# A three-pass mixture of experts on one core: splits of pass 1 put a step later, operands of pass 3 made in pass 2

## Chip, cores and metric

The kernel runs on one core of one Trainium2 chip. The metric is the time of one execution on the device in microseconds (us), lower is better. Before the change it is 2345.62 us, the median of 3 runs (2342.83 to 2346.38).

## What is computed

Attention with a threshold, a gated feed-forward block, and a mixture of eight experts whose gate is normalised over rows and columns eight times. The change concerns the experts alone.

```
attn = softmax(where(scores >= max - tau, scores, -1e9)) @ v
x = (silu(attn @ w_gate) * (attn @ w_val)) @ w_out
P = exp(x @ w_gate2 - max); 8 times: P /= row sums; P /= column sums; P *= N / E
out = sum over e of P[:, e] * (relu(x @ w1[e]) @ w2[e])
N, D, E, F = 2304, 512, 8, 1024
```

## The kernel before

Every product is made of three matmuls in a fast fp32 format: an operand is split into a high half (a copy, on ScalarE) and a low half (the operand less its high half, on GpSimd or VectorE), and high x high, high x low and low x high are added up.

The experts' part runs over the 2304 tokens in three passes (`u` = 0, 1, 2), of two blocks of 384 tokens each. The text calls them pass 1, 2 and 3. A pass has 32 steps (`k`): each takes 256 of the 1024 hidden columns of one of the 8 experts, four steps to an expert (`PAIRS` = 4). In a step the 2 x 2 product of weights and x is made as seven products of sums of quarters. They stand in the order `UP_ORDER` = (1, 2, 6, 5, 7, 4, 3), and the number n of a product names the slot of the step.

Pass 1 (the loop over k from L1664) makes the weights' operands as it goes and stores them in DRAM for passes 2 and 3. `a_steps(k + 1)` makes those of w1 for the next step: three sums on VectorE, then the splits `wa` and `wb`, then s4 (L1095), which writes over a part of what `wa` was made of and so must wait for GpSimd's low half of `wa`, then the split `wc` of s4. `b_steps(k)` splits w2, `t_sums(k)` makes four differences of w2 on VectorE, and `t_steps(k)` splits these a step later, with one low half on GpSimd and one on VectorE. `a_store`, `b_store` and `t_store` write the operands to DRAM. Meanwhile TensorE does the seven up-products of step k (`up`, six matmuls of 384 columns each) and, between them, the products with w2 of step k - 1 (`mix`, six pieces of six matmuls of 512 columns, called y-matmuls here), whose results VectorE adds to the output tiles `acc`. Product 6 is copied to `av` by ScalarE, product 7 to `u3`; products 6, 7 and 4 write the same bank, so product 7 waits for the `av` copy and product 4 for the `u3` copy. Product 3 waits for VectorE's sums with `u3` and `av` (L1328, L1329).

Each engine works in the order in which the program is written. `between(n)` (L1651) sets it: it runs one piece of `mix`, then n of the parts that wait in `w_parts`, and in every second call a step of the gate's normalisation (`sink`, in steps 1 to 9). It is called in each slot but n = 2, after the slot's up-product. `w_some(99)` runs all the parts that are left.

Passes 2 and 3 read the stored weights in two streams, A (w1) and B (w2), each three tiles ahead, and their own operands of x, X11 to Xt4. `x_make(u)` makes these from two blocks of x, in parts: each `op` is a copy on ScalarE and a subtraction on GpSimd or VectorE, each `less` a subtraction on VectorE, and the store of an operand goes out with the next `op` (`keep`). Both `x_make(1)` and `x_make(2)` are run in pass 1, from step 10 on, one part in slot 6 and one in slot 5; `x_make(2)` begins with the load of its x. In the last step `x_fetch` reads pass 2's X back into the slots of pass 1's X. In passes 2 and 3 (`up_gated`, `down_gated`) a step has seven up-products and fourteen half pieces of the down-products, all of six matmuls of 384 columns; the results of an up-product are multiplied by the gate's values `p`, a row of DRAM spread over the partitions by `gates_load`. The s tiles of these passes are sums of such results; they stand in the pool `rw`, which has two buffers.

Large tiles take one of 26 slots (20, and 6 of x). `new` takes the slot that has been free the longest, and `drop` gives one back; a transfer into a slot waits for those who used it last. All transfers go through SP's queue, in order.

Of the kernel before, what the change touches and what calls it, by code (L numbers as in the profile page):

```python
# [11 lines left out]
F32 = mybir.dt.float32  # L12
F32R = mybir.dt.float32r
# [7 lines left out]
P = 128  # L21
BLK = 384
# [110 lines left out]
def attention_moe_moe_kernel(  # L133
# [60 lines left out]
    def copy_act(o, i):  # L194
        nc.scalar.activation(out=o, in_=i, func=AF.Copy)  # L195
# [519 lines left out]
    def new(shape, dt, name):  # L715
        tag = free_slots.popleft()
        t = slots[tag[0]].tile(shape, dt, tag=tag, name=name)
        home[name] = tag
        return t

    def drop(name):
        free_slots.append(home.pop(name))
# [5 lines left out]
    PAIRS = FE // P // 2  # L728
# [15 lines left out]
    for f in range(NF1):  # L744
        for nm, x in (("g", w_gate), ("v", w_val)):
            t = dram.tile([P, CC, P], F32, tag=f"{nm}{f}", name=f"first_{nm}{f}")
# [270 lines left out]

    xo = {}

    def x_op(u, nm, x, eng):  # L1020

        t = new([P, 2, 2, BLK], F32R, f"X{u}_{nm}")
        hi, lo = t[:, 0], t[:, 1]
        xo[u, nm] = hi, lo, t
        copy_act(hi, x)
        eng.tensor_tensor(lo, x, hi.bitcast(F32), op=ALU.subtract)
# [106 lines left out]
    def t_sums(k):  # L1133
        raw = raws.pop(("b", k))
        wt[k] = [new([P, 2, 2, DM // 2], F32R, f"t{k}_{n}") for n in range(2)]
        (b21, b22), (b11, b12) = ((t[:, 0], t[:, 1]) for t in raw)
        (t4, t2), (t1, t3) = ((t[:, 0, 1].bitcast(F32), t[:, 1, 1].bitcast(F32)) for t in wt[k])

        def one():
            nc.vector.tensor_tensor(t1, b12, b11, op=ALU.subtract)  # L1140
            nc.vector.tensor_tensor(t3, b22, b12, op=ALU.subtract)

        def two():
            nc.vector.tensor_tensor(t2, b22, t1, op=ALU.subtract)
            nc.vector.tensor_tensor(t4, b21, t2, op=ALU.subtract)

        yield one
        yield two

    def t_steps(k):  # L1150
        for n, eng in ((1, nc.gpsimd), (0, nc.vector)):
            yield from b_split(wt[k][n], wt[k][n][:, :, 1].bitcast(F32), eng)

    def flat(x):
        return x.bitcast(F32).rearrange("p h a d -> p h (a d)")
# [7 lines left out]
    def t_store(k):  # L1163
        g, x = divmod(k, GROUP)
        f1, f2 = wt.pop(k)
        nc.sync.dma_start(b_kept[g][:, 0:4:3, x], flat(f1))
        nc.sync.dma_start(b_kept[g][:, 2:5:2, x], flat(f2))
        for n in range(2):
            drop(f"t{k}_{n}")
# [5 lines left out]
    rw = ctx.enter_context(tc.tile_pool(name="rw", bufs=2, reuse_waits="tile"))  # L1175
    tmp = ctx.enter_context(tc.tile_pool(name="tmp", bufs=2, reuse_waits="tile"))
# [257 lines left out]
    later = deque()  # L1434
    ops, gates, free_halves, sums7 = {}, {}, deque(), {}

    def gates_load(u, e):
        t = gates[u, e] = tmp.tile([P, 2 * BLK], F32, tag="cv", name=f"p{u}_{e}", bufs=2)
        o = e * NT + 2 * u * BLK
        nc.sync.dma_start(t, p_kept[0, o:o + 2 * BLK].partition_broadcast(P))  # L1440

# [140 lines left out]
    def x_make(u):  # L1582

        if u == 2:
            yield lambda: x_load(u)
        box = {}

        def less(n, m, o):

            def fn():  # L1590
                y = box["y"]
                nc.vector.tensor_tensor(y[n], y[m], y[o], op=ALU.subtract)
            return fn

        def keep():
            nm = box.pop("nm", None)
            if nm is not None:
                kept = xo_kept[u, nm] = dram.tile([P, 4 * BLK], F32, tag=f"kx{u}{nm}", name=f"kx{u}{nm}")
                hi = xo.pop((u, nm))[2]
                nc.sync.dma_start(kept, hi.bitcast(F32).rearrange("p a d n -> p (a d n)"))  # L1600
                drop(f"X{u}_{nm}")

        def op(nm, n, eng):
            def fn():
                keep()
                if "y" not in box:
                    box["y"] = [x[:, y:y + 2] for x in x2[2 * u:2 * u + 2] for y in (0, 2)]
                x_op(u, nm, box["y"][n], eng)
                box["nm"] = nm
            return fn  # L1610

        yield op("11", 0, nc.gpsimd)
        yield op("21", 1, nc.gpsimd)
        yield less(0, 2, 0)
        yield op("22", 3, nc.gpsimd)
        yield less(2, 3, 2)
        yield less(3, 3, 0)
        yield op("t2", 3, nc.vector)
        yield op("t1", 0, nc.gpsimd)
        yield op("t3", 2, nc.vector)  # L1620
        yield less(1, 1, 3)
        yield op("t4", 1, nc.vector)

        def done():
            keep()
            drop(f"x2_{2 * u}")
            drop(f"x2_{2 * u + 1}")

        yield done

    def x_fetch(u, n):

        nm = PARTS[n]
        drop(f"X{u - 1}_{nm}")
        t = new([P, 2, 2, BLK], F32R, f"X{u}_{nm}")
        xo[u, nm] = t[:, 0], t[:, 1]
        nc.sync.dma_start(t.bitcast(F32).rearrange("p a d n -> p (a d n)"), xo_kept[u, nm])
# [3 lines left out]
    w_parts = deque()  # L1641

    def w_some(n):
        for _ in range(n):
            if w_parts:
                w_parts.popleft()()
# [5 lines left out]
    def between(n):  # L1652
        nonlocal sink
        x = next(fill, None)
        if callable(x):
            x()
        w_some(n)
        turn[0] += 1
        if sink is not None and turn[0] % 2 and next(sink, 0) == 0:
            sink = None  # L1660

    x_parts = itertools.chain(x_make(1), x_make(2))

    for k in range(NG):  # L1664
        if k + 2 < NG:
            a_load(k + 2)
        b_load(k)
        a_store(k)
        if k:
            b_store(k - 1)  # L1670
        products = up(k, 0)
        fill = iter([down_last, lambda: logits(4)]) if k == 0 else mix(k - 1, 0)
        if k == 2 * PAIRS + 1:
            while sink is not None:
                between(0)
        if k == NG - 1:
            a_in.begin()
        if k + 1 < NG:
            w_parts.extend(a_steps(k + 1))
        for n in UP_ORDER:  # L1680
            next(products)
            if k == NG - 1:
                x_fetch(1, n)
            if n == 5:
                w_parts.extend(b_steps(k))
            if n == 7 and k:
                w_parts.extend(t_steps(k - 1))
            if n == 3:
                w_some(99)
                if k:  # L1690
                    t_store(k - 1)
                w_parts.extend(t_sums(k))
            if n != 2:
                between(4 if n == 7 else 3)
            if n in (6, 5) and k > 2 * PAIRS + 1:
                next(x_parts, lambda: 0)()
        a_drop(k)
        w_some(99)
        if k:
            wb.pop(k - 1)  # L1700
            for n in range(2):
                drop(f"b{k - 1}_{n}")
        if k == 0:
            logits_t(3)
            logits(5)
            logits_t(4)
            for i in range(4, NBLK):
                nc.sync.dma_start(x_kept[i], x2[i])
                drop(f"x2_{i}")
        if k == 1:  # L1710
            logits_t(5)
            sink = gate_steps()
    for fn in x_parts:
        fn()

    gates_load(1, 0)
    b_store(NG - 1)
    later.extend(t_steps(NG - 1))
    later.append(lambda: t_store(NG - 1))
# [10 lines left out]
    for _ in range(7):  # L1730
        t = new([P, 2, 2, BLK], F32R, f"halves{len(free_halves)}")
# [17 lines left out]
    t = [new([P, 2, 2, BLK], F32, f"sums{x}") for x in range(4)]  # L1749
    sums7.update((n, t[n // 2][:, n % 2]) for n in range(8))  # L1750

    groups = [(u, g) for u in range(1, PASSES) for g in range(NG // GROUP)]
    outs = iter(())
    for (u, g), (u0, g0) in zip(groups[1:], groups):
        downs = down_gated(u0, g0)
        for x in range(GROUP):
            k = GROUP * g + x
            if (k + 1) % PAIRS == 0:
                u1, e1 = divmod((u * NG + k + 1) // PAIRS, E)
                if u1 < PASSES:  # L1760
                    gates_load(u1, e1)
            products = up_gated(u, k)
            for y, n in enumerate(UP_ORDER):
                slot(products)
                if u < PASSES - 1 and k == NG - 1:
                    x_fetch(u + 1, n)
                if x == 0 and y in (0, 2, 4):
                    next(outs, None)
                next(downs)
        for _ in downs:  # L1770
            pass
        if g0 == NG // GROUP - 1:
            outs = turn_out(u0)
# [45 lines left out]
```

## Time and profile before

| | us |
|---|---|
| median of 3 runs | 2345.62 (2342.83 to 2346.38) |
| the profiled execution | 2348.69 |
| its span, first to last instruction | 2346.9 |
| TensorE (PE) busy in the span | 2243.4 (96%) |
| VectorE (DVE) / GpSimd (POOL) / ScalarE (ACT) busy | 1696.3 / 1132.2 / 966.8 |
| pass 1, 32 steps (first up-product to the first of pass 2) | 800.36 to 1367.36 |
| passes 2 and 3 | 1367.36 to the end |

The profile is one execution on the chip. "Busy" is the share of time in which an engine works on an instruction; a timeline row gives start, duration, engine, source line, operation, the output and the inputs, and in brackets the idle time before it and who ended it. A line can be a helper's: L195 is every plain copy of ScalarE. A step of pass 1 begins with the first matmul of up-product 1 (L1291).

### The profile page before, as it was taken

The numbers are of one execution on the slowest core, as the hardware profiler recorded it, in microseconds if no ns is written. First come the engines' busy times: TensorE is split into PE (matmuls) and PEld (weight loads), VectorE is DVE, ScalarE is ACT, GpSimd is POOL, SyncE is SP. The second block draws the span as 40 slices with busy tenths as digits, with TensorE's granted clock in tenths as the row PEclk, the third lists the DMA queues.
The fourth block names the chain that finished last, engine by engine and source line by source line (L and its number), as shares of the span: only waits on it lengthen the run. The fifth ranks groups of instructions, "written<-read, shape, count | busy, mean of one in ns | idle before, by whom it ended". The sixth has DMA issues, their size and how long they took to land.

```text
span 2346.9 us, 35120 instructions
## 1 busy us (share of the span) xinstructions
PE 2243.4 (96%) x12787; PEld 2089.3 (89%) x12787; DVE 1696.3 (72%) x2736; ACT 966.8 (41%) x1847; POOL 1132.2 (48%) x1073
## 2 busy tenths in 40 slices
PE   7999999999999999997999979999999999999998
PEld 6677769999999887786888869999999999999997
DVE  6899978385843378886878856777777857777776
ACT  4777763322223254444444424333333343333332
POOL 4887866454545344554555524444444334444442
PEclk8999999999999999998999989999999999999999
DMA  8666632010200278787898897777777877777774
GB/s 210 149 160 148 154 90 68 26 56 27 62 22 3 86 254 284 254 314 295 299 340 283 297 386 269 261 258 259 259 260 260 320 273 260 261 260 262 258 258 135
DMA packets 214381, 491.56 MB, mean 209 GB/s; under 512 B 56496, under 2 KB 102720, under 8 KB 214208
## 3 DMA queue, kind: packets, MB, share of 16 engines
q1 hardware_dynamic: 214208, 489.32, 63.3%
q8 instruction: 101, 1.65, 0.3%
q14 instruction: 72, 0.59, 0.1%
HBM read 322.72 MB, written 137.18 MB: 196 GB/s over the span
## 4 chain that ended last, share of the span: by engine, by line
PE 70%; DVE 8%; DMA 7%; POOL 5%; issue 5%; SPq 3%; ACT 2%; ACTq 0%; POOLq 0%; DVEq 0%
PE d L845 8%; PE d L847 8%; PE d L846 8%; PE up L1455 6%; PE up L1456 6%; PE up L1457 6%; PE v L845 2%; PE v L847 2%; PE v L846 2%; PE g L845 2%; PE g L847 2%; PE g L846 2%; PE y L847 2%; PE y L846 2%; PE pv L627 1%
## 5 line engine op out<-in xcount | busy, mean ns | idle before, releaser
L1554 DVE TENSOR_TENSOR sums<-d,sums 128x768 f32<-128x768 f32 x210 | 199.4, 950 | 112.1 <-PE d L847 112.1
L1478 POOL TENSOR_TENSOR halves<-s,halves 128x384 fp32r<-128x384 f32 x192 | 245.9, 1308 | 67.2 <-ACT halves L195 65.1
L845 PE MATMUL d<-halves,B 128*128 128x384 f32 x640 | 214.6, 335 | 0.3 <-DVE sums L1554 0.3
L846 PE MATMUL d<-halves,B 128*128 128x384 f32 x640 | 214.2, 335 | 0.0
L1478 POOL TENSOR_TENSOR h<-u,h 128x384 fp32r<-128x384 f32 x64 | 65.8, 1028 | 307.5 <-ACT h L195 149.5
L847 PE MATMUL d<-halves,B 128*128 128x384 f32 x640 | 214.2, 335 | 0.0
L195 ACT ACTIVATE halves<-s 128x384 fp32r<-128x384 f32 x256 | 134.1, 525 | 123.1 <-DVE s L1510 97.5
L990 POOL TENSOR_TENSOR h<-av,h 128x384 fp32r<-128x384 f32 x72 | 88.8, 1234 | 198.1 <-ACT h L195 198.1
L1455 PE MATMUL up<-X_t,A 128*128 128x384 f32 x512 | 171.6, 335 | 6.7 <-ACT u L195 6.6
L1457 PE MATMUL up<-X_t,A 128*128 128x384 f32 x512 | 171.4, 335 | 0.0
L1456 PE MATMUL up<-X_t,A 128*128 128x384 f32 x512 | 171.4, 335 | 0.0
L1478 POOL TENSOR_TENSOR h<-s,h 128x384 fp32r<-128x384 f32 x64 | 65.2, 1019 | 196.4 <-ACT h L195 110.5
L1085 POOL TENSOR_TENSOR wa<-a,wa 128x768 fp32r<-128x768 f32 x32 | 59.5, 1859 | 205.1 <-ACT wa L195 195.2
L847 PE MATMUL y<-b,h 128*128 128x512 f32 x384 | 154.4, 402 | 0.0
L846 PE MATMUL y<-b,h 128*128 128x512 f32 x384 | 153.8, 401 | 0.0
L845 PE MATMUL y<-b,h 128*128 128x512 f32 x384 | 151.9, 396 | 0.0
L986 DVE TENSOR_TENSOR av<-v,s 128x384 f32<-128x384 f32 x72 | 40.0, 556 | 153.1 <-PE v L847 137.7
L479 DVE SCALAR_TENSOR_TENSOR em<-ns,st,ee 128x576 f32<-128x576 f32 x144 | 137.4, 954 | 12.7 <-POOL st L466 8.6
L1455 PE MATMUL up<-X,A 128*128 128x384 f32 x384 | 129.7, 338 | 8.0 <-DMA X<-kx 5.8
L1456 PE MATMUL up<-X,A 128*128 128x384 f32 x384 | 129.3, 337 | 0.0
L1457 PE MATMUL up<-X,A 128*128 128x384 f32 x384 | 129.1, 336 | 0.0
L195 ACT ACTIVATE u<-up 128x384 f32<-128x384 f32 x96 | 46.6, 485 | 198.1 <-PE up L1457 195.0
(598 smaller groups left out, 7160.6 us busy)
## 6 DMA issues: line engine op xcount, KB each, us to landing
A<-ka SPq DMA_DIRECT2D x128, 768.0 KB, 4.3
B<-kb SPq DMA_DIRECT2D x128, 768.0 KB, 6.3
kb<-t SPq DMA_DIRECT2D x64, 512.0 KB, 4.2
ka<-wa SPq DMA_DIRECT2D x32, 768.0 KB, 7.1
ka<-wb SPq DMA_DIRECT2D x32, 768.0 KB, 8.5
kk<-khl SPq DMA_DIRECT2D x64, 320.0 KB, 4.9
b<-in_moe_w_dram SPq DMA_DIRECT2D x64, 256.0 KB, 5.6
kb<-b SPq DMA_DIRECT2D x32, 512.0 KB, 8.4
```

The lines of the kernel that those rows point to most:

```text
L195: nc.scalar.activation(out=o, in_=i, func=AF.Copy)
L479: nc.vector.scalar_tensor_tensor(m, sc.pop(t), stat.pop(t)[:, 1:2], ee.pop(t), op0=ALU.is_le, op1=ALU.mult, accum_out=sums[p][:, s:s + 1],)
L845: nc.tensor.matmul(ps, a[0], b[0], start=start, stop=False)
L846: nc.tensor.matmul(ps, a[0], b[1], start=False, stop=False)
L847: nc.tensor.matmul(ps, a[1], b[0], start=False, stop=stop)
L990: nc.gpsimd.tensor_tensor(h[:, 1], av, h[:, 0].bitcast(F32), op=ALU.subtract)
L1085: yield lambda: nc.gpsimd.tensor_tensor(o[:, :, 1], x, o[:, :, 0].bitcast(F32), op=ALU.subtract)
L1455: nc.tensor.matmul(ps, a[:, 0, d], bh[:, d], start=start and d == 0, stop=False, skip_group_check=True)
L1456: nc.tensor.matmul(ps, a[:, 0, d], bl[:, d], start=False, stop=False, skip_group_check=True)
L1457: nc.tensor.matmul(ps, a[:, 1, d], bh[:, d], start=False, stop=d == 1, skip_group_check=True)
L1478: eng.tensor_tensor(h[:, 1], src, h[:, 0].bitcast(F32), op=ALU.subtract)
L1554: nc.vector.tensor_tensor(sum7(u, n), t[:, :, 0:BLK], sum7(u, n), op=ALU.add)
```

## The change

In pass 1 the parts are handed out two to a slot. `t_steps(k - 1)` is run whole in slot n = 2, which has no piece of `mix`; `b_steps(k)` joins the queue in slot 4 instead of slot 5; `t_store(k - 1)` and `t_sums(k)` stand at the end of the step, behind the last slot. One part of `x_make(1)` is run a step, in slot 5, and `x_make(2)` is moved to pass 2, from step 8 on, one part a step in the third slot. Its operands take a buffer of `rw` (the s tiles' pool) instead of a slot. The first gates of pass 2 are loaded at the start of the last step of pass 1, into a slot of their own.

```diff
-    def x_op(u, nm, x, eng):
-        t = new([P, 2, 2, BLK], F32R, f"X{u}_{nm}")
+    def x_op(u, nm, x, eng, t=None):
+        if t is None:
+            t = new([P, 2, 2, BLK], F32R, f"X{u}_{nm}")
...
-    def gates_load(u, e):
-        t = gates[u, e] = tmp.tile([P, 2 * BLK], F32, tag="cv", name=f"p{u}_{e}", bufs=2)
+    def gates_load(u, e, t=None):
+        if t is None:
+            t = tmp.tile([P, 2 * BLK], F32, tag="cv", name=f"p{u}_{e}", bufs=2)
+        gates[u, e] = t
...
-                drop(f"X{u}_{nm}")
+                if u == 1:
+                    drop(f"X{u}_{nm}")
...
-                x_op(u, nm, box["y"][n], eng)
+                t = rw.tile([P, 2, 2, BLK], F32R, tag="raw", name=f"X{u}_{nm}") if u == 2 else None
+                x_op(u, nm, box["y"][n], eng, t)
...
-    x_parts = itertools.chain(x_make(1), x_make(2))
+    x_parts = x_make(1)
...
         if k == NG - 1:
             a_in.begin()
+            t = new([P, 2 * BLK], F32, "gates")
+            gates_load(1, 0, t)
...
-            if n == 5:
+            if n == 2:
+                for fn in t_steps(k - 1) if k else ():
+                    fn()
+                continue
+            if n == 5 and k > 2 * PAIRS + 1:
+                next(x_parts, lambda: 0)()
+            if n == 4:
                 w_parts.extend(b_steps(k))
-            if n == 7 and k:
-                w_parts.extend(t_steps(k - 1))
-            if n == 3:
-                w_some(99)
-                if k:
-                    t_store(k - 1)
-                w_parts.extend(t_sums(k))
-            if n != 2:
-                between(4 if n == 7 else 3)
-            if n in (6, 5) and k > 2 * PAIRS + 1:
-                next(x_parts, lambda: 0)()
+            between(2)
         a_drop(k)
         w_some(99)
+        if k:
+            t_store(k - 1)
+        for fn in t_sums(k):
+            fn()
...
-    gates_load(1, 0)
     b_store(NG - 1)
...
+    x_parts = x_make(2)
...
+            if (u, k) == (1, PAIRS):
+                drop("gates")
...
+                if u == 1 and k >= 2 * PAIRS and n == 6:
+                    next(x_parts, lambda: 0)()
```

ScalarE in step 25 of pass 1, from the relu of product 2 (`h25_0_11`) on; `av` and `u3` are the copies of products 6 and 7, `wb26` and `wc26` the w1 operands of the next step. Before:

```order
L1304 ACTIVATE h25_0_11_12944<-up25_0_12923 128x384
L195 ACTIVATE av_12954<-up25_0_12916 128x384
L195 ACTIVATE wb26_12914<-a26_12744 128x3x256
L195 ACTIVATE wc26_12915<-a26_12744 128x256
L195 ACTIVATE b25_0_12974<-b25_0_12904 128x2x256
L195 ACTIVATE u3_12993<-up25_0_12916 128x384
L1304 ACTIVATE h25_0_22_12997<-u3_12993 128x384
L195 ACTIVATE b25_1_12975<-b25_1_12905 128x2x256
```

And after:

```order
L1305 ACTIVATE h25_0_11_12900<-up25_0_12880 128x384
L195 ACTIVATE t24_1_12852<-t24_1_12852 128x2x256
L195 ACTIVATE t24_0_12851<-t24_0_12851 128x2x256
L195 ACTIVATE av_12914<-up25_0_12873 128x384
L195 ACTIVATE wb26_12871<-a26_12701 128x3x256
L195 ACTIVATE u3_12949<-up25_0_12873 128x384
L1305 ACTIVATE h25_0_22_12953<-u3_12949 128x384
L195 ACTIVATE wc26_12872<-a26_12701 128x256
L1305 ACTIVATE h25_0_21_12901<-up25_0_12873 128x384
L195 ACTIVATE b25_0_12975<-b25_0_12861 128x2x256
L1305 ACTIVATE h25_0_12_12954<-up25_0_12926 128x384
L195 ACTIVATE b25_1_12976<-b25_1_12862 128x2x256
```

The `wc` copy and the `b` copies have moved behind the `u3` copy, and the two t copies ahead of the `av` copy; the second `b` copy is now the step's last.

SP's queue in the last step of pass 1, from the A stream's second fetch on (`p1_0` and `gates` are the gates' first load, `X1_` the operands of pass 2). Before:

```order
L1414 DMA A1_0_3_13843<-ka0_91 128x1536
L1414 DMA A1_0_6_13845<-ka0_91 128x1536
L1637 DMA X1_11_13856<-kx111_10568 128x1536
L1637 DMA X1_21_13876<-kx121_10730 128x1536
L1637 DMA X1_t2_13886<-kx1t2_11054 128x1536
L1637 DMA X1_t1_13903<-kx1t1_11195 128x1536
L1637 DMA X1_t3_13932<-kx1t3_11357 128x1536
L1637 DMA X1_t4_13954<-kx1t4_11382 128x1536
L1637 DMA X1_22_13973<-kx122_11029 128x1536
L1166 DMA kb15_122<-t30_0_13818 128x2x512
L1167 DMA kb15_122<-t30_1_13819 128x2x512
L1440 DMA p1_0_13991<-kp_125 128x768
```

And after:

```order
L1415 DMA A1_0_3_13800<-ka0_91 128x1536
L1415 DMA A1_0_6_13802<-ka0_91 128x1536
L1443 DMA gates_13804<-kp_125 128x768
L1642 DMA X1_11_13815<-kx111_10713 128x1536
L1642 DMA X1_21_13835<-kx121_11031 128x1536
```

The gates' load has moved from behind nine transfers to ahead of the first X.

SP's queue in pass 2 of the changed kernel, around the first store of an operand of pass 3 (`X2_11`, step 10):

```order
L1415 DMA A1_5_6_15292<-ka5_96 128x1536
L1415 DMA B1_4_6_15309<-kb4_111 128x1536
L1415 DMA A1_5_9_15354<-ka5_96 128x1536
L1603 DMA kx211_15360<-X2_11_15217 128x1536
L1415 DMA B1_4_9_15382<-kb4_111 128x1536
L1415 DMA A1_5_12_15413<-ka5_96 128x1024
```

The stores of pass 3's operands have come in between the fetches of the two streams; before, there was none here.

## Rows read from the trace of the kernel before

**Rows 1.** Busy time in stretches: steps 1-9, 10-30, 31, the joint, pass 2.

```profile
core 0: us, PE busy (x) PEld busy (x) DVE busy (x) ACT busy (x) POOL busy (x), PEclk, DMA share, GB/s
822.06:979.86 157.80, 148.13 (x728) 129.83 (x727) 128.25 (x252) 75.50 (x150) 74.49 (x54) 0.99 0.75 260
979.86:1345.71 365.85, 340.25 (x1639) 300.47 (x1639) 293.04 (x458) 160.28 (x309) 194.08 (x134) 0.97 0.86 305
1345.71:1367.36 21.65, 15.81 (x80) 13.91 (x78) 12.07 (x23) 5.54 (x11) 3.86 (x3) 0.92 0.99 382
1367.36:1403.66 36.30, 28.10 (x126) 25.42 (x126) 17.98 (x30) 11.12 (x23) 11.59 (x10) 0.86 1.02 395
1403.66:1866.00 462.34, 461.95 (x2663) 461.63 (x2664) 339.65 (x483) 158.96 (x320) 184.99 (x158) 1.00 0.79 271
```

**Rows 2.** The same view: step 16, and the three steps 25 to 27.

```profile
1084.93:1113.11 28.18, 18.74 (x80) 16.48 (x78) 13.15 (x22) 8.04 (x15) 10.27 (x7) 0.76 0.73 274
1251.11:1298.03 46.92, 46.92 (x236) 42.16 (x234) 39.16 (x64) 21.27 (x42) 24.67 (x18) 1.00 0.88 303
```

**Rows 3.** Waits of TensorE in pass 1: total us, times, longest.

```profile
PE up L1291 <- ACT u L195: 33.7, 18, 9.4
```

**Rows 4.** Timeline of step 22, all engines.

```profile
1209.54 1.85 POOL L1085 TENSOR_TENSOR wb<-a,wb 128x768 fp32r<-128x768 f32 x1
1209.62 2.05 DVE L1095 TENSOR_TENSOR a<-a 128x256 f32<-128x256 f32 x1 [0.22 <-POOL wa L1085]
...
1211.70 0.42 ACT L195 ACTIVATE wc<-a 128x256 fp32r<-128x256 f32 x1 [2.56 <-DVE a L1095]
...
1211.93 0.39 PE L845 MATMUL y<-b,h 128*128 128x512 f32 x1
1212.02 0.62 ACT L195 ACTIVATE b<-b 128x512 fp32r<-128x512 f32 x1
...
1212.55 0.47 ACT L195 ACTIVATE u<-up 128x384 f32<-128x384 f32 x1
...
1213.32 0.33 PE L1291 MATMUL up<-X_t,wb 128*128 128x384 f32 x1
```

**Rows 5.** Timeline of step 16, ScalarE and TensorE.

```profile
1104.04 0.84 ACT L195 ACTIVATE X<-x 128x768 fp32r<-128x768 f32 x1 [7.59 <-DMA x<-kx]
...
1105.31 0.69 PE L1291 MATMUL up<-X_t,wb 128*128 128x384 f32 x1 [9.44 <-ACT u L195]
```

**Rows 6.** Chain of waits at the joint: start, us, what.

```profile
1357.84 11.27 DMA X<-kx
1369.17 13.28 DMA p<-kp
...
1393.60 9.22 DMA out_dram<-acc
```

**Rows 7.** Timeline of TensorE at the joint.

```profile
1367.36 0.66 PE L1455 MATMUL up<-X,A 128*128 128x384 f32 x1 [5.84 <-DMA X<-kx]
...
1384.16 0.69 PE L1455 MATMUL up<-X_t,A 128*128 128x384 f32 x1 [6.57 <-ACT u L195]
```

**Rows 8.** Groups by line: busy us, mean ns, idle before.

```profile
L1124 POOL TENSOR_TENSOR b<-b,b 128x512 fp32r<-128x512 f32 x64 | 85.6, 1343 | 37.9 <-ACT b L195 36.8 <-issue 1.1
...
L1026 POOL TENSOR_TENSOR X<-x,X 128x768 fp32r<-128x768 f32 x9 | 17.9, 1988 | 17.9 <-ACT X L195 9.7 <-DMA x<-kx 8.2
...
L1592 DVE TENSOR_TENSOR x<-x,x 128x768 f32<-128x768 f32 x6 | 8.9, 1485 | 0.0
```

**Rows 9.** DMA issues of the whole run: count, KB, median us to landing.

```profile
A<-ka SPq DMA_DIRECT2D x128, 768.0 KB, 4.3
...
kx<-X SPq DMA_DIRECT2D x6, 768.0 KB, 8.9
```

**Rows 10.** Timeline of ScalarE in two steps of pass 2.

```profile
1564.84 0.47 ACT L195 ACTIVATE up<-up 128x384 f32<-128x384 f32 x1 [0.36 <-PE up L1457]
...
1573.22 0.49 ACT L195 ACTIVATE u<-up 128x384 f32<-128x384 f32 x1 [3.25 <-PE up L1457]
```

**Rows 11.** Timeline of VectorE in the second of these steps.

```profile
1573.74 0.56 DVE L1502 TENSOR_TENSOR u<-up,u 128x384 f32<-128x384 f32 x1 [2.75 <-ACT u L195]
```

## Prediction

> **What bounds the kernel now.** I read the stretches first [rows 1]. Passes 2 and 3 are TensorE's: from 1403.66 to 1866.00 it is busy for 461.95 of 462.34 us. Pass 1 is not. Three of its steps, 1251.11 to 1298.03, take 46.92 us with TensorE busy throughout [rows 2], so a step that waits for nothing takes 46.92 / 3 = 15.64 us. The 9 steps 1 to 9 take 157.80 us, which is 157.80 - 9 x 15.64 = 17.0 too long; the 21 steps 10 to 30 take 365.85, or 37.4 too long; step 31 takes 21.65, or 6.0 too long. In steps 10 to 30 TensorE is idle for 365.85 - 340.25 = 25.6 of the 37.4; the other 11.8 are matmuls at the lower clock after an idle stretch (granted 0.76 of full speed in the worst step [rows 2], 0.97 over all 21 [rows 1]).
>
> Next, who ends the idle time: the list of waits names one wait, an up-product of TensorE for ScalarE's copy of `u3` [rows 3]. The timeline of step 22 shows the chain behind it [rows 4]. VectorE's s4 (L1095) stands beside GpSimd's low half of `wb` and takes 2.05 us; ScalarE's `wc` waits 2.56 us for s4; a `b` copy follows; only then comes the `u3` copy, at 1212.55. The matmul that needs it starts at 1213.32, behind six y-matmuls that began at 1211.93. So the copy has the 1.39 us of those six in which to finish. Here it just fits; in a step with one operation more ahead of it (an operand of pass 2 or 3, a part of the gate) it doesn't. ScalarE itself is idle most of the time: 160.28 of 365.85 us busy [rows 1]. Late is the order, not the engine.
>
> Two waits are of another kind. In step 16 ScalarE stands 7.59 us before the first operand of pass 3, whose x has just been asked for, and TensorE 9.44 us behind it [rows 5]; that step takes 28.18 us [rows 2], 12.5 too long. At the joint to pass 2 the chain of waits runs over the fetch of the first X, then over the load of the gates `p`, then over an output store [rows 6]; TensorE waits 5.84 us for X and 6.57 us for a copy that stands behind the gates [rows 7].
>
> **Part by part.** The forecast is made against the profiled execution (2348.7 us, span 2346.9 and 1.8 around it). It lies 3.1 above the median of 2345.6, and I move the difference to the median.
>
> Order of pass 1. The `wc` and both `b` copies now stand behind the `u3` copy on ScalarE, s4 stands two slots later on VectorE, and the t splits go to the slot without y-matmuls. Nothing is added. Ahead of the `u3` copy, between the `av` copy and it, there remains the `wb` copy, which is as long as an operand copy, 0.84 [rows 5], and in some steps one operand copy of 0.84; the stretch from the `av` product's end to `u3`'s is two y-pieces of 1.39 and two up-pieces of (15.64 - 6 x 1.39) / 7 = 1.04, 4.9 us. Some 0.5 for the `av` copy and 1.7 for the two fit, with the two t copies of 0.62, the form of the `b` copy in [rows 4], ahead of them. What is late next is VectorE: s4 may still meet `wb` on GpSimd and take 2.05, then the two sums on `u3` stand behind it; but the product that needs them starts 1.39 + 1.04 + 1.39 = 3.8 us after `u3`'s, and 2.05 and two operations of 0.56 [rows 11] fit. VectorE's load of 39.16 / 3 = 13.1 us a step [rows 2] leaves room for one operand part of 1.49 [rows 8]. So in steps 10 to 30 I take away nearly all of the 37.4: the bounds are 12.5 (the x wait alone, below) and 37.4, and I take **34**, leaving 0.3 us for each of the 11 steps that still make an operand. Steps 1 to 9 have 17.0, but VectorE is at 128.25 / 9 = 14.3 us a step there [rows 1], since it also normalises the gate, and TensorE has the gate's small matmuls, 157.80 - 148.13 = 9.7 being all that is idle. Bounds 0 and 9.7; I take **6**.
>
> Pass 3's operands leave pass 1: 13 parts, with seven operands, four subtractions and two loads. With the load goes the wait of step 16, 12.5 us, which is counted in the 34. In pass 2 one part a step is placed in step k's third slot. The parts are four GpSimd subtractions of 1.99, four VectorE ones of 1.49 [rows 8], three more low halves on VectorE, and seven ScalarE copies of 0.84. In the steady part of pass 2 that place is idle: ScalarE waits 3.25 us before its next copy, and VectorE 2.75 [rows 10, 11]. They cost nothing where they land in that hole; without it each would be paid in full, 4 x 1.49 + 3 x 1.49 = 10.4 for VectorE's.
>
> But the seven operands now share the two buffers of the s tiles, and seven s tiles have to wait for an operand's store to land. Three of these stores (steps 10, 12, 16) go out behind an A fetch that itself waits for the third up-product; from its end to the s tile's first write there are six pieces of 1.04, 6.2 us. Three others go out two pieces earlier, and the last has a whole step. An X store lands after 8.9 us in pass 1, where the transfers are denser; an A fetch lands after 4.3 [rows 9]. Issuing takes about 1, and VectorE may be some 0.8 late before TensorE feels it: ScalarE is idle for 0.36 before the next step's first copy [rows 10], and the copy has about 0.5 to spare. At 4.3 the wait costs nothing; at 8.9 it is 8.9 + 1.0 - 6.2 - 0.8 = 2.9 for each of three and 2.9 - 2 x 1.04, about 0.8, for each of the next three, 11 in all. Halfway, at 6.6, it is 0.6 for each of three: I charge **2**, with 0 and 11 as bounds.
>
> The gates. The load now goes out before the first X, into a slot of its own, so the 6.57 us [rows 7] and the lower clock after them go, and the first X lands later by 128 x 768 words, 393 KB, about 1 us at 395 GB/s [rows 1]. But the joint is full: DMA share 1.02 from 1367.36 to 1403.66, and the chain passes from the gates to an output store of 9.22 us [rows 6]. What TensorE doesn't wait for at the gates it may wait for there. Bounds 0 and 7.5; I take **5**. The 5.84 us for X stay.
>
> The store of t at the step's end, and the slots: SP waits less, and the t tiles get slots that were given back a step before. I cost it at nothing, since no row shows TensorE waiting there; SP's queue would show it.
>
> Sum: 34 + 6 + 5 - 2 = 43 us; 2345.6 - 43 = **2303** (the profiled execution 2306).
>
> **Rivals.**
> VectorE is the bound. The order on ScalarE is mended, but VectorE, at 293.04 / 21 = 14.0 us a step [rows 1], comes late to the same products. For it: s4 still meets GpSimd. Against it: VectorE's 13.1 us in the clean steps cost nothing. Then only the x wait and the joint are gained: 12.5 + 5 - 2 = 16, **2330**.
>
> The b splits come too late. They now end the step, and the next step's first y-matmuls read them one up-piece later. From the last up-product's end there are 1.39 + 1.04 + four y-matmuls of 0.23, 3.4 us; a relu of about 0.47, like the copy of its size in [rows 10], the copy of 0.62 and GpSimd's 1.34 [rows 4, 8] need 2.4 and some passing on. If GpSimd is behind by half a microsecond more than I think, 30 steps lose 0.5 each: **2318**.
>
> The lock in pass 2. In step 22 a VectorE subtraction of 256 elements lasts 2.05 us because GpSimd's `wb` runs from 1209.54 for 1.85 [rows 4]: it ends 0.3 after it. If the four GpSimd subtractions of 1.99 hold up VectorE in pass 2 for their full length and the hole doesn't cover it, that is 8.0 us: **2311**. The Trainium skill, page "SBUF — State Buffer", section "SBUF: two separate sides", has this as a rule: GpSimd and a VectorE operation with two SBUF inputs share a port pair, whichever starts first has it for its whole instruction, and the other is blocked altogether. That speaks against new GpSimd work in pass 2; the trace agrees on the block, but not yet on whether it reaches TensorE.
>
> Slower: no free slot in pass 2. There are 26 slots; X has 7, the halves 7, the sums 4, the A and B streams 3 each: 24. The two x tiles take the last two from step 8 to 20, so each A or B fetch must wait for the very tile that TensorE has just left, and has five products, 5 x 2 x 1.04 = 10.4 us, to land. With 4.3 us [rows 9] nothing happens. If the nine added transfers of 768 KB bring the mean landing to 11.2, some 64 fetches pay 0.75 each, 48 us: **2351**. It decides from about 10.4 on; the densest stretch of pass 1 had 8.9 for the same size, so it is unlikely.
>
> Nothing is gained: VectorE is the bound, the joint gives back its 5 and the stores cost 11: 12.5 - 11 = 1.5, **2344**. The change would then not do what it says.
>
> **How the numbers follow.** The forecast (2290 to 2315) has 0.60, the lock 0.08, VectorE 0.12, the b splits 0.08, the slots 0.05, nothing 0.04; 0.03 is for a time under 2290 (37.4, 9.7 and 7.5 gained in full and nothing paid is 55 us, 2291). The range 2288 to 2322 holds the forecast, the lock, the b splits and a part of VectorE's case, 0.8. About 0.2%, 4.7 us, can be told from no change: faster by more has 0.60 + 0.08 + 0.12 + 0.08 + 0.03 = 0.91, the same 0.04, slower 0.05.
>
> **What would show it.** Right: steps 10 to 30 at 15.64 to 16 us, the wait for `u3` gone from the list, step 16 like its neighbours, the wait for `p` gone and that for X still near 6 us, pass 2 as busy as before but for some short waits in steps 10, 12 and 16. Wrong: a wait of y-matmuls for `b`, of up-products for L1329's and L1330's results, idle time in pass 2 that ends with an A or B fetch, or a joint that still ends with the output store at the same distance.

## The result and the profile after

The changed kernel takes 2317.02 us (median of 4 runs, 2316.23 to 2317.57); the kernel before took 2346.00 beside it. The ratio is 0.9874, 95% interval 0.9855 to 0.9893. The forecast was 2303 in 2288 to 2322: the sign and the range hold, but 29 us were gained by the medians where 43 were expected.

The profiled execution took 2316.23 us against 2348.69, 32.5 less. Where these lie is read from the same stretches as before [rows 1]. First the span of the changed kernel, then its stretches, in the order steps 1 to 9, steps 10 to 30, step 31, the joint up to the first down-product, pass 2.

```profile
span 2314.4 us, 35285 instructions
```

```profile
core 0: us, PE busy (x) PEld busy (x) DVE busy (x) ACT busy (x) POOL busy (x), PEclk, DMA share, GB/s
821.08:977.51 156.43, 147.97 (x728) 128.49 (x727) 132.10 (x253) 73.80 (x148) 75.81 (x52) 1.00 0.74 270
977.51:1311.65 334.14, 332.54 (x1639) 295.59 (x1639) 291.33 (x453) 155.96 (x306) 199.66 (x133) 1.00 0.85 312
1311.65:1334.67 23.02, 15.81 (x80) 13.91 (x78) 13.02 (x22) 5.42 (x11) 5.11 (x4) 0.95 0.88 324
1334.67:1367.53 32.86, 28.65 (x126) 25.53 (x127) 18.70 (x29) 10.13 (x21) 11.82 (x10) 0.88 1.00 386
1367.53:1829.87 462.34, 459.36 (x2643) 458.09 (x2644) 339.54 (x486) 164.45 (x329) 192.16 (x162) 1.00 0.82 288
```

| stretch, us | before [rows 1] | after | difference | forecast |
|---|---|---|---|---|
| up to step 1 | 822.06 | 821.08 | -1.0 | 0 |
| steps 1 to 9 | 157.80 | 156.43 | -1.4 | -6 |
| steps 10 to 30 | 365.85 | 334.14 | -31.7 | -34 |
| step 31 and the joint | 57.95 | 55.88 | -2.1 | -5 |
| first down-product of pass 2 to the end | 943.24 | 946.87 | +3.6 | +2 |

The differences add up to 32.5. The 3.5 beyond the medians' difference is that of one execution: the profiled one before stood 2.7 above its median of 2346.0, the one after 0.8 below.

So the large term was nearly right. The list of TensorE's waits in pass 1 and the joint shows it (total us, times, longest; `cs` is the gate's column sum): the 33.7 us of [rows 3] have shrunk to 0.6, and small waits for VectorE and for GpSimd's `b` have taken their place.

```profile
PE up L1458 <- DMA X<-kx: 7.2, 1, 7.2
PE up L1292 <- DVE up L1330: 6.4, 8, 1.9
PE up L1458 <- DMA A<-ka: 3.9, 2, 3.0
PE cs L1257 <- DVE cs L1254: 1.6, 2, 1.3
PE y L846 <- POOL b L1125: 1.3, 3, 0.6
...
PE up L1292 <- ACT u L195: 0.6, 1, 0.6
```

The three small terms are too favourable by 3 to 5 us or (pass 2) too low by 1.6. Each has its rows.

**Steps 1 to 9.** Before, TensorE waited there 8.5 us for `u3`; now it waits 5.9 us for VectorE's sums. The two lists, before and after:

```profile
PE up L1291 <- ACT u L195: 8.5, 5, 2.3
```

```profile
PE up L1292 <- DVE up L1330: 5.9, 7, 1.9
```

VectorE's timeline of step 7 shows what stands between s4 (L1096) and the sum that TensorE waits for (L1330): s4 beside GpSimd's `wb` for 2.05 us as in [rows 4], then four operations of the gate's normalisation (0.83 us), then the two sums.

```profile
935.41 2.05 DVE L1096 TENSOR_TENSOR a<-a 128x256 f32<-128x256 f32 x1 [0.54 <-POOL wa L1086]
937.38 0.15 DVE L1258 TENSOR_SCALAR cs<-cs 128x8 f32<-128x8 f32 x1
937.57 0.20 DVE L1259 RECIPROCAL cs<-cs 128x8 f32<-128x8 f32 x1
937.80 0.17 DVE L1260 TENSOR_SCALAR cs<-cs 128x8 f32<-128x8 f32 x1
938.01 0.31 DVE L1261 TENSOR_TENSOR gate_p<-gate_p,cs 128x144 f32<-128x144 f32 x1
938.23 0.55 DVE L1329 TENSOR_TENSOR u<-up,u 128x384 f32<-128x384 f32 x1
938.70 0.56 DVE L1330 TENSOR_TENSOR up<-up,av 128x384 f32<-128x384 f32 x1
```

TensorE stood 1.45 us for the last of these.

**The joint.** The wait for the gates [rows 6, 7] is gone. In its place TensorE waits 2.97 and 0.91 us for fetches of the A stream, and the first X is 1.4 us later (7.21 us against 5.84):

```profile
1334.67 0.66 PE L1458 MATMUL up<-X,A 128*128 128x384 f32 x1 [7.21 <-DMA X<-kx]
1355.16 0.44 PE L1458 MATMUL up<-X_t,A 128*128 128x384 f32 x1 [2.97 <-DMA A<-ka]
1365.88 0.44 PE L1458 MATMUL up<-X,A 128*128 128x384 f32 x1 [0.91 <-DMA A<-ka]
```

**Pass 2.** VectorE's timeline of step 10: the s tile waits 2.66 us for the store of pass 3's first operand, which was issued at 1489.54 by SP's timeline, some 8.5 us before the s tile was written.

```profile
1494.79 0.55 DVE L1470 SCALAR_TENSOR_TENSOR u<-u,p 128x384 f32<-128x384 f32 x1
1498.00 0.56 DVE L1470 SCALAR_TENSOR_TENSOR s<-up,p 128x384 f32<-128x384 f32 x1 [2.66 <-DMA kx<-X]
```

Steps 12 and 16 show the same with 2.40 and 3.25 us, some 8.2 and 9.1 us after the issue; TensorE stands 0.75, 0.50 and 1.34 us behind the three. In the steady part of pass 2 no row waits for an A or B fetch.

### The profile page after: what moved, and what is told of

It reads as the page before. It is cut to its first block, busy times and chain, and to the rows that moved or that the text cites. A ratio compares the mean times of both kernels' runs of the same rounds, so it can differ in the third digit from the quotient of the medians.

```text
span 2314.4 us, 35285 instructions
## 1 busy us (share of the span) xinstructions
PE 2235.4 (97%) x12787; PEld 2082.2 (90%) x12787; DVE 1702.9 (74%) x2736; ACT 965.2 (42%) x1847; POOL 1147.9 (50%) x1073
## 4 chain that ended last, share of the span: by engine, by line
PE 70%; DVE 11%; POOL 6%; DMA 6%; issue 4%; ACT 2%; SPq 1%; ACTq 0%; POOLq 0%; DVEq 0%
PE d L845 8%; PE d L847 8%; PE d L846 8%; PE up L1458 6%; PE up L1460 6%; PE up L1459 6%; PE v L845 2%; PE v L847 2%; PE v L846 2%; PE g L845 2%; PE g L847 2%; PE g L846 2%; PE s L455 2%; PE pv L627 2%; PE y L846 2%
## 5 line engine op out<-in xcount | busy, mean ns | idle before, releaser
L1505 DVE TENSOR_TENSOR u<-up,u 128x384 f32<-128x384 f32 x64 | 35.7, 558 | 123.6 <-ACT u L195 123.6
```

## Experiments

Each of the first three kernels is the kernel before with one part of the change.

### order_only: the order of pass 1 alone

```diff
+            if n == 2:
+                for fn in t_steps(k - 1) if k else ():
+                    fn()
+                continue
...
+            if n == 4:
+                w_parts.extend(b_steps(k))
+            between(2)
```

(with the t store and sums at the step's end; both `x_make` stay in pass 1, two parts a step)

> The kernel before with the new order of pass 1 alone: both operand makers stay in pass 1, two parts a step, and the gates' load stays where it was. Theory (ScalarE's order made the steps long): the wait of an up-product for the u3 copy goes from all steps but step 16, whose wait for x (9.4 us idle, 12.5 with the lower clock) stays, since the operand copy still stands ahead of the u3 copy. Steps 10 to 30 lose 37.4 - 12.5 - about 5 for two parts a step = 20 us, steps 1 to 9 about 1.4 as in the changed kernel: 2346 - 21 = 2325. Rival (VectorE is the bound, the order only moves the wait): under 5 us gained, 2341 or more, with a wait of the up-product 3 for VectorE's sums in nearly every step from 10 on.

Measured: 2342.41 us, ratio 0.998 (0.997 to 0.9991): the rival's case, under 5 us gained. Steps 10 to 30 take 361.45 us, 4.4 less than before. TensorE's waits in pass 1:

```profile
PE up L1291 <- DVE up L1329: 17.8, 15, 2.0
PE up L1291 <- ACT u L195: 9.0, 4, 6.6
```

The wait for `u3` falls from 33.7 to 9.0, of which 6.6 are step 16 with its load of x. But a wait for VectorE of 17.8 us appears. VectorE's timeline of step 12, which has two operand parts (L1592):

```profile
1024.31 2.60 DVE L1592 TENSOR_TENSOR x<-x 128x768 f32<-128x768 f32 x1
...
1027.50 1.94 DVE L1592 TENSOR_TENSOR x<-x,x 128x768 f32<-128x768 f32 x1
...
1030.02 0.41 DVE L1095 TENSOR_TENSOR a<-a 128x256 f32<-128x256 f32 x1
1030.35 0.55 DVE L1328 TENSOR_TENSOR u<-up,u 128x384 f32<-128x384 f32 x1
1030.82 0.55 DVE L1329 TENSOR_TENSOR up<-up,av 128x384 f32<-128x384 f32 x1
```

And GpSimd's beside it:

```profile
1023.79 2.30 POOL L1085 TENSOR_TENSOR wa<-a,wa 128x768 fp32r<-128x768 f32 x1
1026.06 2.56 POOL L1085 TENSOR_TENSOR wb<-a,wb 128x768 fp32r<-128x768 f32 x1
```

Both parts stand ahead of s4 and the two sums, and each ends 0.82 us after the GpSimd operation that it met (1026.91 after 1026.09, 1029.44 after 1028.62). The order on ScalarE was the wait that ended last; VectorE stood just behind it. The Trainium skill, page "SBUF — State Buffer", section "SBUF: two separate sides", says that GpSimd and a VectorE operation with two inputs in SBUF share a port pair and that one is blocked while the other works; these rows agree, as [rows 4] did for s4.

### x_only: pass 3's operands in pass 2 alone

```diff
-    x_parts = itertools.chain(x_make(1), x_make(2))
+    x_parts = x_make(1)
...
```

(with `x_make(2)` in pass 2, in buffers of `rw`, as in the change)

> The kernel before with the operands of pass 3 made in pass 2, and nothing else changed; operands of pass 2 still two parts a step. Theory: steps 16 to 22 become like those without operand parts; of their excess (12.5 in step 16; 1.3, 4.4, 0.6 and 4.9 in steps 18 to 21) nearly all goes, 22 us, and pass 2 pays the 3.6 us that the changed kernel pays there (waits of an s tile for a store in steps 10, 12 and 16): 2346 - 19 = 2327. Together with the run of the order alone this is more than the changed kernel's 29, because the waits of steps 18 to 21 are in both. Rival (the making costs in pass 2 what it costs in pass 1, lock or load): 2340 or more, with pass 2 over 10 us longer.

Measured: 2330.64 us, ratio 0.9918 (0.9889 to 0.9947). Steps 10 to 30 take 347.03 us, 18.8 less than before, while the order alone gave 4.4 and the whole change 31.7. In the profiles the two together give 31.7 - 18.8 - 4.4 = 8.5 us more in this stretch than the sum of what each gives by itself. The wait that is left is ScalarE's again:

```profile
PE up L1292 <- ACT u L195: 18.3, 12, 4.0
```

### gates_only: the gates' early load alone

```diff
         if k == NG - 1:
             a_in.begin()
+            t = new([P, 2 * BLK], F32, "gates")
+            gates_load(1, 0, t)
...
-    gates_load(1, 0)
```

> The kernel before with the gates' first load moved ahead of the X fetches, and nothing else. Theory (the joint is bound by the bytes that have to move): the wait of 6.6 us behind the gates goes, the wait for the first X grows by about 1.4 us to 7.2, and up-products wait for an A fetch instead, about 4 us; net gain 2 us, 2344. Rival (the gates were the bound at the joint): the 6.6 us and the lower clock after them are gained but for 1 us, 2339 or less.

Measured: 2344.88 us, ratio 0.9994 (0.998 to 1.0007), no difference that this can tell. The wait for `p` is gone; the wait for the first X has grown from 5.84 to 7.2 us, and two waits for A fetches are new:

```profile
PE up L1457 <- DMA X<-kx: 7.2, 1, 7.2
PE up L1457 <- DMA A<-ka: 6.0, 2, 3.3
```

With a DMA share of 1.02 at the joint [rows 1] the order of the transfers only decides which one is waited for. What helps is fewer of them there (x_ahead, below).

The other kernels are edits of the changed one; each asks for one of the small terms.

### s4_later: VectorE's s4 behind the two sums

```diff
-            between(2)
+            between({5: 1, 4: 3}.get(n, 2))
```

> The changed kernel with one part moved: s4 runs on VectorE behind the two sums on u3 instead of ahead of them, the splits behind it move one place on. Theory (in steps 1 to 9 up-product 3 waits for VectorE's second sum, because s4 ahead of it stands 2 us beside GpSimd's low half of wb): the 6.4 us of that wait go, and with the lower clock after them 6 to 9 us; s4 takes 0.4 instead of 2.05 us where GpSimd is through: 2317 - 7 = 2310. Rival (VectorE has too much work in the gate's steps, wherever s4 stands): the wait only moves, under 2 us gained, 2315 or more.

Measured: 2327.32 us, ratio 0.9916 (0.9896 to 0.9937), 10 us worse than the change, for a reason that neither the theory nor the rival named. The wait for the sums falls from 6.4 to 2.6, but the y-matmuls now wait for the `b` splits, and steps 12 to 21 take about 16.4 us each:

```profile
PE y L846 <- POOL b L1125: 7.9, 24, 0.9
...
PE up L1292 <- DVE up L1330: 2.6, 3, 1.6
```

With s4 later, `wc` is later, and the `b` splits stand behind `wc`. The rival of late `b` splits was refuted for the change itself (1.3 us in all) but lies less than a microsecond a step away.

### wc_last: the same, with the `wc` split behind the `b` splits

```diff
-                w_parts.extend(b_steps(k))
-            between(2)
+                w_parts.extendleft(reversed(list(b_steps(k))))
+            between({5: 1, 7: 1}.get(n, 2))
```

> The changed kernel with s4 behind the two sums on u3, as in the run s4_later, but with the wc split at the end of the step, behind the b splits, so that these are no later than in the changed kernel. Theory (s4_later lost by b splits that came late for the next step's y-matmuls): the waits of y-matmuls for b go (7.9 us there, 24 times), steps 11 to 21 take 15.6 to 15.9 instead of 16.4, step 10 loses its 21.3; with steps 1 to 9 as in s4_later (157.6 us): 2316 or a little less, the same as the changed kernel. Rival (s4_later lost because s4 itself stands worse there): 2322 or more.

Measured: 2315.46 us (2309.26 to 2316.26), ratio 0.9861 (0.9839 to 0.9884). By the profile steps 1 to 9 take 153.92 us, 2.5 less than the change, and steps 10 to 30 take 332.27, 1.9 less. The profiled execution is the 2309.26, the other three stand at 2315.43 to 2316.26: by its median the edit can't be told from the change.

### t_gpsimd: VectorE's low half of t given to GpSimd in steps 2 to 8

```diff
-        for n, eng in ((1, nc.gpsimd), (0, nc.vector)):
+        for n, eng in ((1, nc.gpsimd), (0, nc.gpsimd if 1 <= k < 2 * PAIRS else nc.vector)):
```

> The changed kernel with both low halves of t on GpSimd in steps 2 to 8, where the gate is normalised; VectorE has one operation of about 1.4 us less in each. Theory (VectorE's load makes these steps long, wherever s4 stands): steps 2 to 8 shorten by 0.7 us each, 5 us, 2312, and the wait of up-product 3 for VectorE's second sum falls from 6.4 to under 3 us. Rival (s4's place behind GpSimd's low half of wa sets it): GpSimd is later by 1.3 us with wa, s4 too, and the steps are as long or longer: 2317 to 2322.

Measured: 2322.11 us, ratio 0.9895 (0.9876 to 0.9915); steps 1 to 9 take 161.63 us, 5.2 more than the change. VectorE has 10.3 us less to do there (121.76 against 132.10), and yet TensorE waits 10.6 us where it waited 8.5, and is busy for 3.0 us more at a granted clock of 0.98 against 1.00. GpSimd's timeline of step 4, then VectorE's:

```profile
879.25 2.55 POOL L1125 TENSOR_TENSOR t<-t 128x512 fp32r<-128x512 f32 x2 [6.41 <-DVE h L1306]
881.76 1.85 POOL L1086 TENSOR_TENSOR wa<-a,wa 128x768 fp32r<-128x768 f32 x1
```

```profile
883.64 2.05 DVE L1096 TENSOR_TENSOR a<-a 128x256 f32<-128x256 f32 x1 [2.63 <-POOL wa L1086]
```

The second t pushes `wa` back, and s4 waits for `wa`: 16.6 us in these nine steps, where it waited 6.5. The gate's parts and the sums stand behind s4. In this step TensorE waits 2.09 us for the gate's column sum, 1.33 in the changed kernel; over the nine steps its wait for the sums is about the same, 5.3 against 5.9. So VectorE's load isn't the bound in these steps; the moment at which s4 can start counts.

### gate_once: one round of the gate's normalisation

```diff
-        for _ in range(8):
+        for _ in range(1):
```

> The changed kernel with one round of the gate's normalisation in place of eight (seven rounds are left out). Theory: the gate alone keeps steps 5 to 9 long; then steps 5 to 9 take 15.7 to 16 each, steps 1 to 9 about 156.4 - 12 = 144 to 146, and the time is about 2305 us, 12 below the changed kernel. Rival: the order (s4 beside wb, operand splits) is what costs there, and the gate only stands beside it; then steps 5 to 9 stay at 17 or more and the time at 2313 to 2317.

Measured: 2306.36 us, ratio 0.9826 (0.9801 to 0.9851). Steps 1 to 9:

```profile
821.87:969.70 147.83, 144.40 (x714) 127.88 (x713) 115.63 (x191) 75.77 (x151) 77.68 (x53) 0.99 0.79 286
```

8.6 us less than with eight rounds. Steps 5, 7 and 8, which held nothing of the gate any more, take 15.64. So the gate is what lengthened them, and the order of the splits was not. The kernel leaves work out, so it is no version to keep. Step 9 is the exception: a wait of 2.10 us for L1330 stays near its end.

### store_early: the operand's store three slots after its making

```diff
...
+                if u == 1 and k > 2 * PAIRS and n == 4:
+                    keeps[2]()
```

> The changed kernel, but in pass 2 an operand's store goes out in the sixth slot of the step that made it, not with the next operand. Theory (what pass 2 lost is an s tile's wait for a store that has just gone out): VectorE's waits of 2.4 to 3.3 us for a store in steps 10, 12 and 16 go, and with them TensorE's 0.75, 0.50 and 1.34 us and the lower clock after them: 3 us, 2314. Rival (pass 2 lost by load on VectorE and GpSimd): no gain, 2317.

Measured: 2314.95 us, ratio 0.9866 (0.9842 to 0.989). From the first down-product to the end 942.9 us, as before the change; VectorE's s in step 10 follows at once:

```profile
1498.16 0.56 DVE L1470 SCALAR_TENSOR_TENSOR s<-up,p 128x384 f32<-128x384 f32 x1
```

The 3.6 us of pass 2 are thus the stores' alone: the parts themselves cost nothing there, and the GpSimd subtractions didn't hold VectorE up in a way that reaches TensorE. This rests on the profiles; the runs (2312.47 to 2317.14) overlap those of the change.

### x_ahead: four of pass 2's X fetched in steps 24 to 30

```diff
...
+        if k in {24: 1, 26: 2, 28: 6, 30: 5}:
+            x_fetch(1, {24: 1, 26: 2, 28: 6, 30: 5}[k], True)
```

(into slots that pass 3's operands no longer take; step 31 then fetches the other three)

> The changed kernel with four of pass 2's seven X fetched at the start of steps 24, 26, 28 and 30 instead of in step 31, into slots that are free there. Theory (the joint is bound by the bytes that must move in it, 22 MB in 56 us): 3.1 MB less make it shorter by up to 7.9 us; the wait for the first X (7.2 us) goes, the waits for A (3.9 us) go or shrink: 2317 - 9 = 2308. Rival (the joint waits for single transfers in a row, the gates, the output stores): only the X wait moves to another, under 3 us gained, 2314 or more.

Measured: 2310.22 us, ratio 0.9844 (0.9825 to 0.9863). Step 31 and the joint:

```profile
1310.75:1326.39 15.64, 15.64 (x80) 14.05 (x78) 10.61 (x17) 5.43 (x11) 3.87 (x4) 1.00 0.89 339
1326.39:1359.95 33.56, 26.76 (x127) 23.63 (x125) 20.84 (x34) 10.43 (x21) 13.06 (x11) 0.95 0.97 362
```

The wait of 7.2 us for the first X is gone, and the joint is only 0.7 us longer: one wait of 1.30 us for a later X is new, and those for A fetches come to 5.2 us in place of 3.9. Step 31 and the joint take 6.7 us less in all. The 3 MB that are fetched where there is room need not be fetched where there is none.

### two_mends, three_mends, gate_spread: the edits together

`two_mends` is store_early and x_ahead; `three_mends` has wc_last as well; `gate_spread` has all three, and hands the normalisation out one part a step, in slot 1, from step 2 on:

```diff
-        if sink is not None and turn[0] % 2 and next(sink, 0) == 0:
+        if sink is not None and turn[0] % 6 == 1 and next(sink, 0) == 0:
...
-        if k == 2 * PAIRS + 1:
+        if k == NG - 2:
             while sink is not None:
                 between(0)
...
```

The second piece changes the lines that, in the changed kernel, end the normalisation before step 9 makes use of it.

> The changed kernel with the early store of pass 3's operands and the four X of pass 2 fetched ahead, both shown alone before. They act in different places (the store in steps 10, 12 and 16 of pass 2, the fetch at the joint), so the gains should add: 2317.0 - 2.1 - 6.8 = 2308 us, with steps 1 to 9 at 156.4, step 31 at 15.6 and 943 us from the first d to the end. Rival: the gains overlap, because transfers moved off the joint or out of the steady part press on others; then about 2310, like the fetch alone.

> The same with s4 behind the u3 sums and the wc split last as well, shown alone at 2315.5 by its runs and a span of 2307.5 in its profile. Steps 1 to 9 should go from 156.4 to 154 and steps 10 to 30 from 334.1 to 332.3, so 2308 - 4.3 = 2304 us (2301 to 2308). Rival: that third edit gained nothing by its median; then it ties with the two edits at 2308.

> Three edits as before, and one part of the gate's normalisation in a step (slot 1, steps 2 to 23) in place of three. Theory: what is left in steps 4 to 9 (154 us against 9 x 15.64 = 140.8) is the gate's three parts a step, whose VectorE operations push s4 and the u3 sums back; spread out, one part of about 0.5 us fits in VectorE's idle time. Steps 1 to 9 go to about 146, steps 10 to 23 lose at most 0.2 each: about 2299 us. Rival: VectorE has nothing to spare there with s4 beside wb, so the cost only moves into steps 10 to 23, which become 16.2 or so: no gain on the three edits, 2304 or slower.

| | us, median | ratio to before (95%) |
|---|---|---|
| two_mends | 2305.12 | 0.9819 (0.9795 to 0.9843) |
| three_mends | 2302.82 | 0.9813 (0.9791 to 0.9835) |
| gate_spread | 2296.52 | 0.9784 (0.976 to 0.9808) |

The gains of the store and the fetch add up: 11.9 us by the medians, where the two alone gave 2.1 and 6.8; the intervals don't set the sum and the measurement apart. The third edit is worth 2.3 us here, and its runs (2301.12 to 2305.76) overlap those without it: it isn't told apart. Spreading the gate is worth 6.3 us, runs 2295.26 to 2297.53. Its steps 1 to 9, with every part of the normalisation still computed, by step 22:

```profile
823.19:970.10 146.91, 143.64 (x715) 127.29 (x714) 110.51 (x203) 75.51 (x147) 77.13 (x53) 1.00 0.80 290
```

Against three_mends, whose steps 1 to 9 take 153.88, that is 7.0 us less, and they don't come back later: steps 10 to 30 take 332.40 us against its 332.70. But it isn't the same computation. Pass 1 multiplies by the gate from step 9 on (L1386, first at 955.0 here), and the last division by column sums (L1261) is at 1135.7, in step 20; in the changed kernel it is at 948.6, ahead of the first use at 961.7. So gate_spread weights pass 1 with a gate that isn't finished. It shows what the place of the parts costs, and is no version to keep; of the kernels here that finish the gate first, three_mends has the lowest median, 2302.82, not told apart from two_mends.

## Why the prediction was right, and where its sizes were off

- **What bounds pass 1: right, but half the cause.** The `u3` copy behind `wc` and `b` on ScalarE was the wait, and the change took it away. Not seen was that VectorE, with two operand parts a step, was late by almost as much: order_only shows it. The VectorE rival was thus true of the new order with the old number of parts, and false of the change because half of the parts leave pass 1. The prediction counted that move for the x wait of step 16 only; x_only shows it worth 18.8 us in steps 10 to 30. So the term of 34 came out near its size by two causes, of which the prediction had one and a part of the other.
- **Steps 10 to 30, 34: measured 31.7.** Of the 5.7 us left over, 2.7 are in step 10, 0.7 in step 12, and six steps with an operand part (14 to 16, 18 to 20) have 0.37 each, about the 0.3 that were set aside. Step 10 was not foreseen: the `b` splits for it come late, behind what delays the end of step 9 (the last section). The prediction also put all of the 11.8 us of extra busy time in these steps down to the lower clock; step 10 of store_early is busy for 16.74 us, 1.1 above a clean step, at a granted clock of 1.00, so a part of it needs no lower clock. The sum didn't use this split.
- **Steps 1 to 9, 6: measured 1.4.** This is the term that failed most. The prediction took ScalarE's order for the cause here too, "since it also normalises the gate" being only a reason to take less. The 8.5 us of waits for ScalarE did go, but 5.9 us for VectorE's sums stood behind them. gate_once and gate_spread show the gate's parts as the cause of most of that: they stand between s4 and the sums on VectorE and, as two small matmuls, in TensorE's own order.
- **Joint, 5: measured 2.1.** The first X came 1.4 later, where 1 was forecast. The gates' wait went, and A fetches took 3.9 us of it back: the upper bound had been named and the place of the next wait was right in kind (a transfer), but it was an A fetch and not the output store. By itself this part is worth nothing measurable (gates_only).
- **Pass 2, +2: measured +3.6.** Steps 10, 12 and 16 waited, and no others, as worked out. That the size was near is in part luck. From the store's issue to the s tile's write there are 8.2 to 9.1 us, where the prediction had 1.0 + 6.6 = 7.6, so VectorE waited longer than was worked out. But VectorE could be late by 1.9 us before TensorE felt it (2.66 - 0.75, 2.40 - 0.50, 3.25 - 1.34), where the prediction had 0.8. The two errors nearly cancel.
- **Rivals.** Late `b` splits: 1.3 us in pass 1, not 15; at full clock they cost step 10 alone some 1.6 us (the last section). The lock in pass 2: hidden (store_early). No free slots: no A or B fetch was waited for in the steady part, though their medians rose in the run as a whole, from 4.3 to 4.9 us for A's 768 KB:

```profile
A<-ka SPq DMA_DIRECT2D x128, 768.0 KB, 4.9
```

One thing is read but not tested: step 9 ends with a wait of about 2 us for the second sum in the kernels with the new order, gate or no gate. VectorE's timeline of the changed kernel has six operations there that stand nowhere else, those of L1386 (the last falls into step 10): they multiply the results of the second expert by the gate and add them to `acc`. Four stand ahead of s4. Two of these meet GpSimd's `wa` and `wb` and take 2.34 and 1.48 us, where 0.75 is normal:

```profile
969.47 2.34 DVE L1386 SCALAR_TENSOR_TENSOR acc<-second,gate_p,acc 128x512 f32<-128x512 f32 x1
...
972.58 1.48 DVE L1386 SCALAR_TENSOR_TENSOR acc<-second,gate_p,acc 128x512 f32<-128x512 f32 x1
```

gate_once has the same two, with 2.34 and 1.47 us. No run moves them.

## What to carry to other kernels

Where several engines feed one product, take the wait that ended last away on paper and look in the trace for the operation that would end next: here it stood just behind, on another engine, and the new order alone was worth 4.4 of the 31.7 us. Small work that is handed out between large parts costs by its place in the order, not by its busy time: the same normalisation cost 6 us less at one part a step than at three. Such work can only be spread as far as its first reader allows, and in this kernel that is step 9. Where transfers fill a stretch, fetch early whatever has a free slot; reordering them moves the wait to another line.

## What was not expected of the hardware

Nearly the same wait was followed by a lower clock in some profiles and by none in others, and the step behind it was as long either way. At the end of step 9 TensorE waits 1.91 us in the changed kernel and 1.92 in store_early, whose edit acts only in pass 2. Step 10 of the two:

```profile
977.51:995.88 18.37, 17.83 (x80) 14.93 (x80) 16.11 (x25) 9.90 (x20) 12.91 (x9) 0.91 0.71 259
979.13:997.63 18.50, 16.74 (x80) 13.87 (x79) 16.24 (x25) 9.93 (x20) 13.04 (x9) 1.00 0.72 257
```

The granted clock was 0.91 in the first and 1.00 in the second. In both the `b` splits come late for the y-matmuls of step 10. At the full clock TensorE stands for them, at the lower clock its matmuls are longer and it stands less (the changed kernel, then store_early):

```profile
PE y L846 <- POOL b L1125: 0.5, 1, 0.5
PE y L846 <- POOL b L1125: 1.6, 2, 0.9
```

So the lower clock cost next to nothing here, since another wait stood behind it. It costs where none does: step 10 of three_mends took 19.69 us at 0.91, against 18.12 at 1.00 in wc_last, with the same 1.8 us of waits for `b`. What decides whether the clock falls after such a wait, no run here shows; in gate_spread the wait was 2.26 us and it stayed at 1.00.

At the joint, where the granted clock is 0.88 over the stretch, the chain of waits has the single matmuls, which show the two levels after the wait of 2.97 us: 0.32 us each at 1.2 GHz, then 0.18 at 2.4 GHz.

```profile
1359.19 0.32 PE up L1460
...
1359.76 0.18 PE up L1459
```

So the waits of TensorE that the list adds up are not what the time would gain without them: a lower clock behind a wait can add to its cost, and it can also vanish in the next wait.
